# Planning a kernel's streams with a longer issue time for turning DMAs, and a new step order to go with it

## The chip, the cores and the metric

The kernel runs on one core of a Trainium2 chip. The metric is the device time of one execution in microseconds (us). PE is TensorE, PEld its weight load, DVE VectorE, ACT ScalarE, POOL GpSimd, SP SyncE; SPq is SyncE's queue of DMA issues.

## The reference

Linear attention with a learned feature map, whose output is the input of a mixture of eight experts with Sinkhorn-normalised routing:

```python
# batch 8, heads 8, seq 576, head_dim 64, features 128
def phi(x):
    proj = einsum('bhsd,df->bhsf', x, w_phi)
    proj = proj - max(abs(proj), axis=-1, keepdims=True)
    return concatenate([exp(proj), exp(-proj)], axis=-1)
q_p, k_p = phi(q), phi(k)
kv = einsum('bhsf,bhsd->bhfd', k_p, v);  z = sum(k_p, axis=2)
attn = einsum('bhsf,bhfd->bhsd', q_p, kv) / (einsum('bhsf,bhf->bhs', q_p, z) + 1e-6)

x = attn.transpose(0, 2, 1, 3).reshape(4608, 512)
P = exp(x @ w_gate - max)                 # 4608 x 8, then 8 rounds of row and column norms
out = sum over e of P[:, e] * (relu(x @ w1[e]) @ w2[e])     # w1: 8 x 512 x 1024
```

## The kernel before

The kernel holds a planner. Each part of the program calls `plan.op(engine, duration, ...)`; a greedy scheduler with a model of durations and of DMA bandwidth then decides the order in which operations are written into each engine's stream, and which buffer each takes. On the chip each engine works through its stream in the order written, and semaphores decide when the next may start. So a duration in the plan costs nothing on the chip; it only decides an order.

```python
LINK = {..., 230: (470, 108), ..., 148: (265, 30), 160: (540, 50)}      # rate: GB/s, share unit

def dma(queue, nbytes, rate, fn, r=(), w=()):
    speed, unit = LINK.get(rate, (rate, 40))
    if nbytes == 2 << 20:
        speed, unit = 400, 150
    o = plan.op(queue, 0.8 if queue == "POOL" else 0.6, 0.0, fn, r, w, (), nbytes / speed)
    o.turn, o.unit = rate == 148, unit
...
class Links:                              # two lines of transfers: SyncE's and POOL's
    def step(self, t, work):
        ...
        if len(on) == 2:
            a, b = (x[0][2] for x in self.line)
            all_ = (0.61 if a.turn else 0.84) / (a.unit + b.unit)
```

The attention's inputs come in halves of a batch (four heads). POOL loads q and k of a half into one of two `qk` buffers by two DMAs, which also turn fp32 into bf16; SyncE loads v; and one "turning" DMA, `dma_start_transpose`, 512 KB from SBUF to SBUF, turns the half so that the features can be computed. A `qk` buffer is free again when its turn has landed.

```python
ring(a_in, [128, 2, 4, NJ * D], BF16, "qk", 2)       # two buffers
ring(a_t, [128, 2, 8, 128], BF16, "qkT", 3)

def load_qk(b, hh, nh, t, r=()):
    ...
    for x, src in ((1, k), (0, q)):
        dma("POOL", nh << 17, 230, lambda ...: nc.gpsimd.dma_start(
            out=t["qk"]()[:, x, o:o + nh], in_=src[b, hh:hh + nh, 0:SM]...), r, ...)

def turn_qk(t, pr=None):
    ...
        dma("SP", 1 << 19, 148, lambda: nc.sync.dma_start_transpose(
            out=t["T"]()..., in_=t["qk"]()...), ...)
```

Smaller turns of the same kind are `rT` (remainders of the sequence) and `xT` (attention output).

The planner's other input is a string of 322 letters, the order in which the steps are offered to the scheduler: `l` loads a half, `t` turns one, `e` loads remainders, `w` loads weights, `a q p r b n m c` are attention steps, `u` and `d` are up and down parts of expert 0, `g` is a routing gate. Only work up to the last gate is ordered by it; the rest of expert 0 and experts 1 to 7 follow.

The softmax here doesn't subtract the row's maximum and nothing guards it: scores larger than these inputs give would overflow.

Of the kernel before, what the change touches and what calls it, by code (L numbers as in the profile page):

```python
# [119 lines left out]
class Links:  # L120
# [13 lines left out]
    def step(self, t, work):  # L134
        on = [n for n in range(2) if self.line[n] and self.line[n][0][0] <= t + 1e-9]
        later = [x[0][0] for n, x in enumerate(self.line) if x and n not in on]
        if not on:
            return (min(later), None, None) if later else None
        share = [1.0, 1.0]
        if len(on) == 2:  # L140
            a, b = (x[0][2] for x in self.line)
            all_ = (0.61 if a.turn else 0.84) / (a.unit + b.unit)
            share = [all_ * a.unit, all_ * b.unit]
        dt, n = min((work[n] / share[n], n) for n in on)
        if later and later[0] - t < dt:
            dt, n = max(later[0] - t, 0.0), None
        for i in on:
            work[i] -= dt * share[i]
        return t + dt, n, work
# [167 lines left out]
def kernel(  # L317
# [59 lines left out]
    plan = Plan()  # L377
# [17 lines left out]
    def dma(queue, nbytes, rate, fn, r=(), w=()):  # L395

        speed, unit = LINK.get(rate, (rate, 40))
        if nbytes == 2 << 20:
            speed, unit = 400, 150
        o = plan.op(queue, 0.8 if queue == "POOL" else 0.6, 0.0, fn, r, w, (), nbytes / speed)  # L400
        o.turn, o.unit = rate == 148, unit

    TI, GR, KM, QM, PM, NM, RM = 0, 0, 0, 0, 0, 0, 0
# [61 lines left out]
    def load_w(e, r=()):  # L465
        w1, w2 = new("w1"), new("w2")
        for w, src in ((w1, moe_w1), (w2, moe_w2)):
            dma("POOL", 2 << 20, 280, lambda w=w, src=src: nc.gpsimd.dma_start(
                out=w(), in_=src[e].rearrange("(c p) f -> p c f", p=128)),
                r, [(w, i, j) for i in range(2) for j in range(2)])  # L470
        return w1, w2

    def load_w0(i, r):

        w1, w2 = W[0]
        n = i % 4
        if i < 4:
            dma("POOL", 1 << 19, 270, lambda: nc.gpsimd.dma_start(
                out=w1()[:, n, :], in_=moe_w1[0].rearrange("(c p) f -> p c f", p=128)[:, n, :]),
                r, [(w1, n)])  # L480
        else:
            dma("POOL", 1 << 19, 280, lambda: nc.gpsimd.dma_start(
                out=w2()[:, 2 * n:2 * n + 2, :],
                in_=moe_w2[0].rearrange("(c p) f -> p c f", p=128)
                [:, 2 * n:2 * n + 2]), r, [(w2, n)])
# [496 lines left out]
    for b in range(2):  # L982
# [4 lines left out]
        w=["wphi_f0"])  # L987
    dma("ACT", 1 << 15, 100, lambda: nc.scalar.dma_start(out=wphi_f[64:128, :], in_=w_phi),
        w=["wphi_f1"])
# [13 lines left out]
    for i in range(2):  # L1003
        dve(450, lambda i=i: nc.vector.memset(vrd[i], 0.0),
            w=[("vrd", i, h, *y) for h in range(2) for y in ((), (1,))])
# [35 lines left out]
    def stage_g(b):  # L1041
# [9 lines left out]
             "c": lambda j: pair_c(j // 4, j % 4, xbs[j]), "g": stage_g,  # L1051
             "u": lambda i: up0(i // 4, i % 4), "d": lambda i: down0(i // 4, i % 4)}
    order = (
        "lraeaepqbwlqaqawwabwmqlltnrbppnwqbppmrmanbqaqmwwacmpnpbccpwbtcnmqnaqbclupunm"
        "taumquglcapalbcpnqqdcenmucugbblnapmrcqdutabnqpmunpbambccddnqplanmqmducpblttb"
        "augnaqlnrbdcampcadmqeutunqcppmdcaqtdqabpbbmlrqtdnpmuaqualbnagnacctbmqulupran"
        "tdpmtdqcmdnpdabdancpcabbqmpumqbcdgnappqunburqcbugmmnqdcdanumupqbnucmcpnmbddp"
        "bqmpncncubncmmgccg"
    )
    for i, n in enumerate(order):  # L1060
        at[0] = i
# [22 lines left out]
    o = plan.op("X", 0.0, 0.0, swap, w=["late"])  # L1084
# [450 lines left out]
```

## Time and profile before

| | before |
|---|---|
| times, us | 1026.58, 1027.88, 1027.87 |
| span of the profiled execution, us | 1026.8 |
| start of the last gate's 32 matmuls, us from the span's start | 204.83 |
| issue of the 12 big turns, us: mean, median, shortest to longest | 2.62, 1.87, 1.32 to 4.51 |
| least time from a big turn's landing to PE's first use of it (loading it as weights), us | 0.7 |

How to read the views: the page's rows of digits are busy tenths in 40 slices of the span; a windows line is "from:to length, then busy us (count) of PE, PEld, DVE, ACT, POOL, then granted clock, DMA share, GB/s"; a row of waits is "engine, what it wanted, its line <- what ended the wait: us in total, times, longest"; a timeline line is "start, duration, engine, line, operation, output <- input, count, and in brackets how long the engine stood idle before it and what released it".

### The profile page before, as it was taken

The page shows a single profiled execution, that of the slowest core. Times are in us where ns is not written, and L with a number is a line of the kernel's source. Part 1 is how long each engine was busy: PE and PEld are TensorE (multiplying, and loading weights), DVE is VectorE, ACT ScalarE, POOL GpSimd, SP SyncE. Part 2 cuts the span into 40 slices and gives each one's busy share as a digit, 9 for nine tenths or more (in the row PEclk, how much of TensorE's full clock was granted, in tenths as well). Part 3 has the DMA queues.
Part 4 walks back from the last instruction along what each step waited for, and adds up shares of the span by engine and source line. Part 5 has one row for each costly group of instructions (what it writes and reads, how often), then busy time and mean ns, then how long its engine had stood idle before and what let it go on. Part 6 is the DMA issues. An engine that isn't in the chain of part 4 may idle for free.

```text
span 1026.8 us, 24281 instructions
## 1 busy us (share of the span) xinstructions
PE 1008.1 (98%) x9469; PEld 837.9 (82%) x9504; DVE 823.5 (80%) x1600; ACT 703.9 (69%) x1530; POOL 458.5 (45%) x480
## 2 busy tenths in 40 slices
PE   7899999999999999999999999999999999999998
PEld 4666666645888888888888888888888888888886
DVE  7999989987888887787777877787778877787775
ACT  7999999834888766666666666666665666666663
POOL 5768664400334444444444434544444433444342
PEclk9999999999999999999999999999999999999999
DMA  9999978170232611161115211341116111614333
GB/s 235 192 197 179 177 137 130 37 154 19 85 104 85 124 42 42 47 129 43 48 46 112 54 43 42 75 102 42 42 46 131 42 42 43 130 36 125 133 124 124
DMA packets 112501, 96.03 MB, mean 94 GB/s; under 512 B 54145, under 2 KB 87041, under 8 KB 112385
## 3 DMA queue, kind: packets, MB, share of 16 engines
q1 hardware_dynamic: 80576, 70.55, 26.5%
q0 software_dynamic: 31648, 23.86, 16.6%
q8 instruction: 74, 1.21, 0.5%
q14 instruction: 43, 0.34, 0.1%
q10 hardware_dynamic: 160, 0.07, 0.0%
HBM read 94.98 MB, written 14.16 MB: 106 GB/s over the span
## 4 chain that ended last, share of the span: by engine, by line
PE 93%; ACT 2%; DVE 1%; DMA 1%; SPq 1%; issue 1%; POOL 0%; DVEq 0%; ACTq 0%
PE ps L1273 74%; PE ps L573 17%; PE ps L856 2%; DMA acc<-in_q_dram 1%; ACT q L569 1%; ACT k L569 0%; SPq L495 0%; ACT wx L569 0%; SPq L551 0%; PE ps L885 0%; DMA xd<-S 0%; DVE ps L864 0%; DVE hT L1305 0%; DVE m L565 0%; POOL wx L761 0%
## 5 line engine op out<-in xcount | busy, mean ns | idle before, releaser
L1428 POOL TENSOR_TENSOR acc<-acc,V 128x512 f32<-128x512 f32 x248 | 314.8, 1280 | 484.5 <-ACT V L1425 426.7
L1301 ACT COPY U<-ps 128x512 f32<-128x512 f32 x378 | 217.0, 586 | 166.2 <-PE ps L1273 150.9
L1305 DVE CUSTOM_DVE_ANT_0 hT<-ps,U 128x512 bf16<-128x512 f32 x378 | 254.6, 687 | 87.7 <-PE ps L1273 59.9
L1425 ACT ACTIVATE V<-ps,P 128x256 f32<-128x256 f32 x496 | 208.1, 473 | 90.7 <-PE ps L1273 82.1
L1413 DVE SCALAR_TENSOR_TENSOR acc<-ps,P,acc 128x256 f32<-128x256 f32 x372 | 159.1, 478 | 69.5 <-PE ps L1273 69.2
L1273 PEld LDWEIGHTS <-S 128*128 128x128 bf16 x1984 | 194.1, 98 | 22.6 <-issue 0.2
L1273 PEld LDWEIGHTS <-T 128*128 128x128 bf16 x1512 | 148.0, 98 | 17.2
L1273 PEld LDWEIGHTS <-hT 128*128 128x128 bf16 x1488 | 145.6, 98 | 16.8
L1273 PE MATMUL ps<-X,T 128*128 128x256 bf16 x1008 | 152.4, 273 | 0.0
L1273 PE MATMUL ps<-T,S 128*128 128x256 bf16 x1056 | 135.8, 273 | 0.0
L1273 PEld LDWEIGHTS <-wx 128*128 128x128 bf16 x1152 | 112.7, 98 | 13.6 <-issue 0.2
L1181 DVE TENSOR_TENSOR S<-hT 128x1024 bf16<-128x1024 bf16 x124 | 87.2, 712 | 10.1 <-ACT hT L1310 9.9
L1273 PEld LDWEIGHTS <-w 128*128 128x128 bf16 x864 | 84.5, 98 | 9.8
L1273 PE MATMUL ps<-xT,wx 128*128 128x256 bf16 x576 | 88.4, 273 | 0.1
L1273 PE MATMUL ps<-X,wx 128*128 128x256 bf16 x576 | 86.8, 273 | 0.0
L1310 ACT ACTIVATE hT<-ps 128x512 bf16<-128x512 f32 x126 | 73.2, 606 | 9.8 <-PE ps L1273 9.8
L1273 PE MATMUL ps<-wx,hT 128*128 128x256 bf16 x560 | 77.6, 273 | 0.0
L1273 PE MATMUL ps<-xT,T 128*128 128x256 bf16 x504 | 76.7, 273 | 0.0
L573 PE MATMUL ps<-xT,w 128*128 128x512 bf16 x270 | 70.5, 379 | 0.7
L573 PE MATMUL ps<-w,hT 128*128 128x512 bf16 x276 | 69.8, 379 | 0.7 <-ACT q L569 0.2
L1273 PE MATMUL ps<-T,hT 128*128 128x256 bf16 x496 | 69.2, 273 | 0.0
L1273 PE MATMUL ps<-xT,w 128*128 128x256 bf16 x432 | 66.5, 273 | 0.0
(129 smaller groups left out, 1426.5 us busy)
## 6 DMA issues: line engine op xcount, KB each, us to landing
X<-xd SPq DMA_DIRECT2D x126, 256.0 KB, 2.7
wx<-in_moe_w_dram POOLq DMA_DIRECT2D x8, 1024.0 KB, 12.4
v_m<-in_v_dram SPq DMA_DIRECT2D x15, 512.0 KB, 5.6
out_dram<-acc SPq DMA_DIRECT2D x14, 512.0 KB, 2.9
w<-in_moe_w_dram POOLq DMA_DIRECT2D x6, 1024.0 KB, 12.1
xd<-S SPq DMA_DIRECT2D x18, 256.0 KB, 2.1
qk<-in_k_dram POOLq DMA_DIRECT2D x12, 256.0 KB, 5.5
qk<-in_q_dram POOLq DMA_DIRECT2D x12, 256.0 KB, 6.4
```

The lines of the kernel that those rows point to most:

```text
L569: act(el, lambda: nc.scalar.activation(out=dst(), in_=src(), func=ACT.Exp, bias=0.0, scale=scale), r, w)
L573: nc.tensor.matmul(out_, lhsT=lhsT, rhs=rhs, start=start, stop=stop)
L856: pe(65, lambda j=j: nc.tensor.matmul(pn()[:, j * D1:j * D1 + D1], lhsT=s["T"][x]()[:, j % 2, 2 * h + j // 2, :] if j < 4 else r["T"][x]() ...
L1181: lambda: f.tensor_tensor(out=out_(), in0=x(), in1=y(), op=op), r, w, **kw)
L1273: pe(256, lambda i=i, k=k, z=z: nc.tensor.matmul(bank()[:, 256 * i:256 * i + 256], lhsT=lhs(k, i), rhs=rhs(k), start=first and z, stop=k = ...
L1301: act(512, lambda: nc.scalar.copy(out=u[fp][n]().rearrange("p a b -> p (a b)"), in_=x[fp]()), [x[fp]], [u[fp][n]])
L1305: dve(515, lambda: nc.vector._custom_dve(ADD_SAT, out=out_(fp, i, j), in0=bank[fp]().rearrange("p (a b) -> p a b", a=2), in1=u[fp][n](), s ...
L1310: act(512, lambda: nc.scalar.activation(out=out_(fp, i, j), in_=x[fp]().rearrange("p (a b) -> p a b", a=2), func=ACT.Relu, bias=0.0, scale ...
L1413: dve(320, lambda n=n, ts=ts: nc.vector.scalar_tensor_tensor(out=acc[g][:, ts, 256 * j:256 * j + 256], in0=bank()[:, 256 * n:256 * n + 256 ...
L1425: act(370, lambda n=n: nc.scalar.activation(out=u()[:, n, :], in_=bank()[:, 256 * n:256 * n + 256], func=ACT.Copy, bias=0.0, scale=P[:, 4 ...
L1428: pool(695, lambda: nc.gpsimd.tensor_tensor(out=acc[g][:, 2 * i:2 * i + 2, 256 * j:256 * j + 256], in0=acc[g][:, 2 * i:2 * i + 2, 256 * j: ...
```

## The change

Its intent: SyncE spends 1.3 to 4.5 us on issuing a big turn where the plan holds 0.6. So the plan gets 2.4 us for the big ones and 1.25 for the small ones, a smaller share of bandwidth while a turn and a load of POOL are in flight together, and a step string that was searched for with these numbers.

```diff
-            all_ = (0.61 if a.turn else 0.84) / (a.unit + b.unit)
+            all_ = (0.56 if a.turn else 0.84) / (a.unit + b.unit)
...
-        o = plan.op(queue, 0.8 if queue == "POOL" else 0.6, 0.0, fn, r, w, (), nbytes / speed)
+        dur = 0.8 if queue == "POOL" else 0.6 if rate != 148 else 2.4 if nbytes > 1 << 18 else 1.25
+        o = plan.op(queue, dur, 0.0, fn, r, w, (), nbytes / speed)
...
     order = (
-        "lraeaepqbwlqaqawwabwmqlltnrbppnwqbppmrmanbqaqmwwacmpnpbccpwbtcnmqnaqbclupunm"
+        "lraplqabaeenqblwqarwamqwppawwbbmpqapwqnqmbpmnmblltanbtcqccncpwnrlwmlucapunmc"
         ... (four more lines replaced in the same way; the same letters in the same numbers)
```

No instruction is added or removed.

More of the change, by code (lines that the diff above doesn't have):

```diff
@@ L1053 @@
     order = (
-        "lraeaepqbwlqaqawwabwmqlltnrbppnwqbppmrmanbqaqmwwacmpnpbccpwbtcnmqnaqbclupunm"
-        "taumquglcapalbcpnqqdcenmucugbblnapmrcqdutabnqpmunpbambccddnqplanmqmducpblttb"
-        "augnaqlnrbdcampcadmqeutunqcppmdcaqtdqabpbbmlrqtdnpmuaqualbnagnacctbmqulupran"
-        "tdpmtdqcmdnpdabdancpcabbqmpumqbcdgnappqunburqcbugmmnqdcdanumupqbnucmcpnmbddp"
-        "bqmpncncubncmmgccg"
+        "lraplqabaeenqblwqarwamqwppawwbbmpqapwqnqmbpmnmblltanbtcqccncpwnrlwmlucapunmc"
+        "gtupabqttlcbmunnqrbecupaaamdgntqdpmaqdbnlbpqaucaalpqmncuaqubapnecqtmcluabnlb"
+        "pmmduaptndglbqpmdaqcdcrqumtbbqnnpqcacttmdapuqbbupnuclrmmmgdbuqnpqanbdcpqmdua"
+        "cmppqndnbccanduarqtdbgnbpacmqunummddapuqbcpacdqbbpgrcnmubmmuunpbdmqnnpabcmcd"
+        "cndqucpmngbpncmccg"
     )
```

## The prediction

> **What bounds the kernel now.** I read the page first, then the time windows of every engine, then the timeline of SyncE's queue, then the list of waits, and at the end the start times of the matmuls. The times of before are 1026.58, 1027.88 and 1027.87 us, so the scatter is about 1.3 us and 2% is 20.6 us.
>
> The page's rows of busy time show three stages. Columns are 40 slices of 25.7 us.
>
> ```profile
> span 1026.8 us, 24281 instructions
> PE   7899999999999999999999999999999999999998
> DVE  7999989987888887787777877787778877787775
> ACT  7999999834888766666666666666665666666663
> PEclk9999999999999999999999999999999999999999
> ```
>
> In slices 2 to 8 (to about 206 us) TensorE, VectorE and ScalarE are all nearly full: this is the attention, mixed with the first part of expert 0. Then ScalarE falls to 3 for two slices: the routing table is made and the rest of expert 0 runs. From slice 10 on experts 1 to 7 run with TensorE always busy at the full granted clock. The windows give the same with numbers (length, then busy us of PE, PEld, DVE, ACT, POOL):
>
> ```profile
> 0.00:50.00 50.00, 38.49 (x398) 26.97 (x400) 43.54 (x90) 43.39 (x109) 31.59 (x58) 1.00 1.15 212
> 50.00:206.00 156.00, 153.69 (x1833) 102.77 (x1861) 143.73 (x340) 147.27 (x358) 101.68 (x163) 1.00 0.90 143
> 206.00:253.00 47.00, 46.77 (x233) 22.46 (x236) 35.96 (x94) 18.18 (x32) 0.62 (x1) 1.00 0.39 85
> 253.00:1027.00 774.00, 769.15 (x7010) 685.69 (x7009) 600.32 (x1078) 495.04 (x1034) 324.63 (x260) 1.00 0.30 76
> ```
>
> The reader should see that 774 of 1027 us lie behind 253 us, where TensorE alone decides; the step order that is changed there is none. What can move is the first 206 us. In that stretch the busy shares of three engines are 92 to 98%, so no single wait carries it.
>
> What SyncE does in that stretch is in its queue's timeline (start, duration, instruction). [...]
>
> ```profile
> 45.39 6.37 SPq L518 DMA_TRANSPOSE qkT<-qk  x2
> 84.84 1.36 SPq L518 DMA_TRANSPOSE qkT<-qk  x1
> 100.38 1.19 SPq L879 DMA_TRANSPOSE xT<-wx  x1
> 116.00 4.51 SPq L518 DMA_TRANSPOSE qkT<-qk  x1
> 141.24 0.37 SPq L509 DMA_DIRECT2D v_m<-in_v_dram  x1
> 171.84 1.69 SPq L518 DMA_TRANSPOSE qkT<-qk  x1
> ```
>
> A plain load costs SyncE 0.37 to 1 us, a turning DMA of a 128 x 512 tile 1.19, and one of 128 x 2048 from 1.32 to 4.51 (the twelve have a mean of 2.6 and a median of 1.87). The plan of before holds 0.6 for all of them. So 34 turning DMAs (12 big, 6 of rT, 16 of xT) take about 12 x 2.6 + 6 x 2.1 + 16 x 1.27 = 64 us of SyncE where the plan thought 20.
>
> Did that hurt? In the list of waits up to 206 us, these are all the rows in which a compute engine's wait was ended by a DMA for 0.2 us or more:
>
> ```profile
> PE ps L703 <- DMA acc<-in_k_dram: 3.7, 1, 3.7
> PEld L573 <- DMA rT<-qk_r: 1.7, 1, 1.7
> ACT wgate L1009 <- DMA wgate_f<-in_moe_w_gate_dram: 0.6, 1, 0.6
> DVE wphi L995 <- DMA wphi_f<-in_w_phi_dram: 0.6, 1, 0.6
> PE ps L703 <- DMA acc<-in_q_dram: 0.3, 1, 0.3
> POOL wx L759 <- DMA xT<-xb: 0.2, 1, 0.2
> ```
>
> The first is the first load of the program. Only rT (1.7 us) and xT (0.2 us) are turning DMAs that came too late for a compute engine, 1.9 us together. SyncE's own waits are long, but its queue has slack: 64 us of issuing in the 165 us from 27 to 192 us.
>
> **What the Trainium skill says.** "DMA: Bandwidth & Descriptors", section "DMA Transpose (X-bar)": the plain DMA transpose can only be issued by Sync or Scalar. That fits the program: every turning DMA stands in SyncE's queue, and there is one queue in which a slow issue delays the v loads behind it. The same page, section "Issuing engines are not separate DMA queues", says that the sequencer's time to start a DMA is usually small against the DMA itself. The trace doesn't agree for turning DMAs: 1.2 of 3.2 us (xT) and a median of 1.87 of 5.9 us from issue to landing (qkT), a third of it. "Trainium Kernel Development and Optimization", section "Performance Expectations", calls matmul busy time a bad metric of the distance to roofline, because matmuls are pipelined. The trace agrees: a 128 x 512 matmul is shown as 379 ns, but 49 of them start in 10.35 us, 211 ns each. So I count TensorE by start-to-start times and not by its 98%.
>
> **The change part by part.** (1) Two durations of SyncE's issue in the plan (2.4 us for the 512 KB turn, 1.25 for the smaller ones) and one bandwidth share (0.56 in place of 0.61). None of this is an instruction; it only changes in what order the planner writes operations into each engine's stream and which buffer and bank each takes. Cost on the chip: 0.
> (2) The string of 322 steps. Both strings have the same letters in the same numbers (32 pairs, 24 up and 20 down parts of expert 0, 12 big turns, 14 half loads, 8 weight loads). The built programs have the same number of instructions on each engine, of the same kinds: PE 18938, DVE 1602, ACT 1534, POOL 485, SP 252. So work removed 0, added 0, all moved. The streams differ from PE instruction 21, DVE 10, ACT 12, SP 19 on; by line and shape the last 462 of ACT, 518 of DVE and 4794 or more of PE are the same again: all from expert 1 on, the 774 us.
>
> What is moved, as work in front of landmarks, with start-to-start times of the trace (512 columns 0.215 us, 256 columns 0.109, 65 columns 0.029; ScalarE 0.476 per 512 elements; VectorE 0.6 per 512 from PSUM):
> - In front of the last gate: PE 179.9 us before, 180.5 after (three more up matmuls); ACT 181.0 in both, with the same 52 relus and 10 copies; VectorE 177 in both. That gate runs at 205.2 us, so about 25 us of each engine are idle in front of it, and behind it the same 47 us of expert 0 cover the routing. The change is worth exactly what it takes from, or adds to, these 25 us.
> - Of PE's idle time in front of the gate, 20.7 us lie in the first 50 us (29.3 us of work there, by the start times), where there is no xT yet to feed expert 0. The first up matmul has 25.9 us of PE work and 39.9 us of ACT work in front of it before, 26.4 and 40.7 after: ScalarE, which is the full engine there, gets 0.8 us more to do first. So this part is +0.3 to +0.8 us.
> - From 50 to 206 us PE loses some 10 us in many small pieces. There the new order spreads expert 0 more evenly. PE work between every 24 up matmuls was 11.6, 18.8, 19.7, 27.4, 9.7, 28.6, 13.5, 18.9 and is 11.5, 22.1, 13.0, 23.7, 19.3, 18.9, 19.1, 19.9. More even filler between work that waits for ScalarE should save a part of the 10 us; I take a quarter at most, -2.5 to 0.
> - The turning DMAs that came late: 1.9 us at most, and part of it would be hidden behind other work; -1 to 0.
> - The fourth quarter of expert 0's first weight is issued with 25.2 us of POOL work in front of it (19.6 before, when it was issued at 35.35 us). I estimate issue at 38 to 41 us; with the page's 7.7 us from issue to landing it lands at 46 to 49, and PE needs it with 28.0 us of work in front of it, so at about 48.5. That is 0 to +1 us.
> Sum of the middles: +0.5 - 1.25 - 0.5 + 0.3 = about -1 us, and with 1027.5 as the centre of before, 1026.5 us.
>
> **The rivals.** (a) The wrong issue times were what made SyncE's queue late and the whole attention slow; then the new order wins several us, to about 1020. For it: 64 us against 20 is a large error, and the queue is in order. Against it: compute engines waited 1.9 us for turning DMAs. (b) The new order is best in the plan alone, and on the chip the streams, which are in order on each engine, meet other waits (a weight that lands late, a bank not yet free), each of which holds three engines; 1029 to 1032. For it: the order is searched against a model with errors as large as the one it now repairs. Against it: the order of before came from the same kind of search and shows few waits. (c) The two orders are two equal solutions, and the difference is within 1 us: 1027 to 1028. (d) The freed time is eaten behind the gate: not likely, since PE is busy 46.77 of 47 us there, so an earlier gate shifts everything.
>
> **Range and chances.** The floor is set by ScalarE: 181 us of work in front of the gate plus about 4 us until its first data, against 205; even a perfect order can't win 20 us, so over 2% faster is next to impossible, and a loss of 20 us would need a new stall almost as long as all idle time there is. From rivals (a) and (b), each with a fifth, the range for 8 in 10 is 1022.5 to 1030.0 us. Chances: faster 0.005, within 2% 0.985, slower 0.01.
>
> **What would show it.** Right: the matmuls from expert 1 on start earlier or later by the same amount as the end; in the windows the stage 253 to 1027 keeps its 774 us; the last gate runs between 202 and 208 us; SyncE's turning DMAs keep 1.2 and about 1.9 us, since the plan's numbers don't change the chip; the waits that DMA end stay under 3 us beside the first load. Wrong: the gate moves by over 5 us, a wait of PE for a weight or a turn of over 2 us appears near 48 us or later, or experts 1 to 7 change in length.

## More of the kernel before

POOL, the engine that issues the q and k loads, also computes: it multiplies v by the features' scale and, before that, negates a small table of maxima (`m_r`, `m`) that ScalarE's next exponential reads.

```python
pool(8, lambda: nc.gpsimd.tensor_scalar_mul(m()[:, 1], m()[:, 2], -1.0), mk, [(m, "neg")])
exp(10, lambda: em(), lambda: m()[:, 1:3], 1.0, mk + [(m, "neg")], [em])
```

The profiled execution of before took 1028.55 us, a little more than the timed ones.

## The result, and the profile after

| | before | after |
|---|---|---|
| median of six runs, us | 1027.2 (1026.36 to 1027.88) | 1030.46 (1029.23 to 1031.09) |
| ratio to before | | 1.003, 95% 1.0017 to 1.0043 |
| span of the profiled execution, us | 1026.8 | 1028.8 |
| start of the last gate's 32 matmuls, us | 204.83 | 206.58 |
| issue of the 12 big turns, us: mean, median, range | 2.62, 1.87, 1.32 to 4.51 | 3.47, 3.27, 1.70 to 6.77 |

The changed kernel is 0.3% slower: within 2%, but 0.46 us above the range that I gave, and its interval excludes 1.

From the page of after, the rows of busy tenths of DVE and ScalarE:

```profile
DVE  7989998887888887788777877787778877787775
ACT  7989998934878766666656666666666666666663
```

In slice 3, which is 51 to 77 us, both fall from 9 to 8; ScalarE also has an 8 in slice 7 where it had a 9. From slice 11 on, where experts 1 to 7 run, the rows differ by one digit in one place (DVE) and in three (ScalarE). In the page's chain of what ended last, PE has 90% of the span where it had 93%. DMA has 3% where it had 1%, and the page's next line gives 2% of them to a turning DMA (`qkT<-qk`) and 1% to a load of q into its buffer (`qk<-in_q_dram`), neither of which was named in the chain before. That names the suspects, no more: time in the chain is not time lost.

Where the time went is shown by short windows. In before:

```profile
65.00:80.00 15.00, 14.68 (x172) 9.81 (x174) 14.10 (x34) 14.19 (x36) 9.01 (x14) 1.00 1.14 192
125.00:150.00 25.00, 24.79 (x267) 15.63 (x269) 23.15 (x53) 24.56 (x65) 17.41 (x32) 1.00 0.82 148
```

In after:

```profile
65.00:80.00 15.00, 13.13 (x136) 8.16 (x137) 12.69 (x29) 12.37 (x31) 11.22 (x19) 1.00 1.43 191
125.00:150.00 25.00, 23.89 (x282) 16.03 (x286) 22.48 (x54) 23.19 (x58) 14.76 (x25) 1.00 1.18 177
```

In the 15 us from 65 us PE loses 1.55 us of busy time against before, DVE 1.41 and ScalarE 1.82, all three at once; POOL is busier by 2.2. In the second window PE loses 0.90, DVE 0.67 and ScalarE 1.37. Elsewhere after is not behind: PE is busy 1.0 us longer in the first 50 us. From the last gate to the end both take nearly the same (821.9 and 822.2 us), so what is lost in front of the gate is lost at the end.

What ended the waits in the first 206 us, where before had no wait of a compute engine for `qkT` or `qk` of 0.2 us or more, is in these rows of after:

```profile
POOL qk L502 <- DMA qkT<-qk: 3.4, 2, 1.7
PEld L574 <- DMA qkT<-qk: 2.3, 2, 1.3
ACT em_r L570 <- POOL m_r L679: 2.0, 2, 1.4
PE ps L574 <- DMA qkT<-qk: 1.9, 2, 1.0
```

PE waits twice for a turn, about 1 us each. POOL waits twice to issue a load of q and k, because the turn that frees the buffer has not landed. ScalarE waits for POOL's negation `m_r`. SyncE's queue in after shows why:

```profile
54.56 0.37 SPq L510 DMA_DIRECT2D v_m<-in_v_dram  x1
56.01 10.05 SPq L519 DMA_TRANSPOSE qkT<-qk  x2
...
129.33 6.21 SPq L519 DMA_TRANSPOSE qkT<-qk  x1
```

The line with x2 holds two issues, of 6.77 and 3.11 us in the trace; the turns land at 66.40 and 69.64 us. The turn of 129.33 takes 6.21 us to issue and lands at 139.04. The plan held 2.4 us for each. What stood waiting, on PE, POOL and ScalarE of after:

```profile
66.45 0.61 PE L574 MATMUL ps<-wphi,qkT 128*128 128x256 bf16 x4 [1.03 <-DMA qkT<-qk]
139.09 1.05 PE L574 MATMUL ps<-wphi,qkT 128*128 128x256 bf16 x8 [0.84 <-DMA qkT<-qk]
```

```profile
66.93 0.77 POOL L502 DMA_DIRECT2D qk<-in_k_dram  x1 [1.69 <-DMA qkT<-qk]
...
70.17 0.74 POOL L502 DMA_DIRECT2D qk<-in_k_dram  x1 [1.72 <-DMA qkT<-qk]
...
71.67 0.25 POOL L679 TENSOR_SCALAR m_r<-m_r 128x4 f32<-128x4 f32 x1
```

```profile
71.95 0.21 ACT L570 ACTIVATE em_r<-m_r 128x8 f32<-128x8 f32 x1 [1.42 <-POOL m_r L679]
```

Read from below: ScalarE stands 1.42 us for a 0.25 us negation, which stands in POOL's stream behind four loads that cost 0.75 us each, two of which waited for late turns. Two turns have no slack at all in after (66.40 landed, 66.45 used; 139.04 and 139.09). The smallest slack of the others is 3.6 us, and two small turns that are issued ahead of the late one at 129 us have 21 and 39 us. Before, the smallest slack of a big turn is 0.7 us (landed at 51.72, loaded as weights at 52.39) and the next 3.4: one turn was nearly late there too, but none was.

### The profile page after: what moved, and what is told of

Read it like the earlier page. It is cut to its first block, busy times and chain, and to the rows that moved or that the text cites. A ratio compares the mean times of both kernels' runs of the same rounds, so it can differ in the third digit from the quotient of the medians.

```text
span 1028.8 us, 24264 instructions
## 1 busy us (share of the span) xinstructions
PE 1008.5 (98%) x9466; PEld 837.4 (81%) x9504; DVE 822.7 (80%) x1600; ACT 704.0 (68%) x1530; POOL 458.2 (45%) x480
## 4 chain that ended last, share of the span: by engine, by line
PE 90%; ACT 3%; DMA 3%; DVE 1%; issue 1%; POOL 1%; SPq 0%; DVEq 0%; ACTq 0%; POOLq 0%
PE ps L1274 74%; PE ps L574 15%; DMA qkT<-qk 2%; PE ps L857 1%; ACT wx L570 1%; ACT k L570 1%; DMA qk<-in_q_dram 1%; ACT q L570 0%; DMA acc<-in_q_dram 0%; ACT qr L570 0%; ACT kr L570 0%; ACT qkT L712 0%; SPq L552 0%; POOL qk_r L557 0%; DVE S L1182 0%
```

## The experiments

**Theories.** The one I held first (theory A in the expectations): the new order leaves two turns with little slack, and as their issue takes longer than the plan's 2.4 us they come late and delay PE. Rivals: the new order is worse by itself, late turns or not (its first 50 us, its filler; theory B); the new numbers alone spoil the plan (theory C in the expectations); and two that came up on the way: the length of an issue is set by what else is in flight, so that no constant fits (theory D), and the loss runs through POOL's in-order stream to ScalarE rather than through PE's own wait (theory E).

**How the edits are made.** After the planner has made its list, a step moves single operations of SyncE or POOL within their streams; (queue, n, m) moves the n-th in front of the m-th. It refuses a move that breaks a dependence or the order of uses of a buffer. PE's, DVE's and ScalarE's streams stay those of the kernel edited.

```diff
+    MOVES = [("SP", 35, 34), ...]
+    def moved(self, done):
+        lists = {q: [o for o in done if o.eng == q] for q in ("POOL", "SP")}
+        for q, n, m in self.MOVES:
+            o, p = lists[q][n], lists[q][m]
+            done.remove(o)
+            done.insert(done.index(p), o)
+        ...                                    # asserts on dependences and buffer order
     def run(self, tc):
-        done = self.schedule()
+        done = self.moved(self.schedule())
```

All twelve kernels gave correct results. "Gate" is the start of the last gate's last matmul in the one profiled execution, "rest" what follows to the end.

| run | median us | before beside it | ratio to before, 95% | gate | rest |
|---|---|---|---|---|---|
| before | 1027.2 | | | 205.6 | 821.2 |
| after | 1030.46 | 1027.2 | 1.003 (1.0017 to 1.0043) | 207.4 | 821.4 |
| newplan_oldstring | 1028.45 | 1027.31 | 1.0004 (0.9988 to 1.0019) | 203.6 | 821.1 |
| oldplan_newstring | 1038.78 | 1026.98 | 1.0114 (1.0101 to 1.0127) | 214.9 | 820.9 |
| after_s1 | 1033.3 | 1027.31 | 1.0055 (1.004 to 1.007) | 210.3 | 820.9 |
| after_s1b | 1029.94 | 1027.31 | 1.0024 (1.0009 to 1.0039) | 208.5 | 820.9 |
| after_s12 | 1034.18 | 1027.31 | 1.0066 (1.005 to 1.0082) | 210.4 | 821.4 |
| after_m | 1030.49 | 1026.98 | 1.0031 (1.0019 to 1.0043) | 208.1 | 820.9 |
| after_msp | 1028.62 | 1026.98 | 1.0014 (1.0002 to 1.0026) | 205.0 | 821.4 |
| after_buf | 1027.85 | 1026.98 | 1.0006 (0.9995 to 1.0018) | 205.8 | 820.7 |
| after_sp | 1028.84 | 1026.97 | 1.0018 (1.0005 to 1.0032) | 207.5 | 821.4 |
| after_buf_sp | 1025.82 | 1026.97 | 0.9986 (0.9974 to 0.9999) | 204.0 | 820.6 |
| after_quiet | 1026.15 | 1026.97 | 0.9991 (0.9978 to 1.0003) | 204.8 | 820.6 |
| before_late | 1032.36 | 1026.97 | 1.0043 (1.0028 to 1.0057) | 210.2 | 821.1 |

The rest lies between 820.6 and 821.4 us in all fourteen profiles: nearly everything that the change and the experiments do to the time happens in front of the gate. A gate time comes from one execution, though, and executions differ: newplan_oldstring, which is nearly the program of before, had its gate 2.0 us earlier in its profile, and that execution took 1026.54 us where the profiled one of before took 1028.55. ScalarE, with the same stream, was 1.2 us ahead at 30 us and 1.6 at 50 us.

### newplan_oldstring: the numbers alone

The new durations and share with the string of before. The built program differs from before in two neighbouring issues of SyncE that are exchanged.

```diff
 (before, with the two hunks of numbers of the change; the string left as it was)
```

> The new numbers in the plan with the old step string. In the built program only two neighbouring SyncE issues change places, so this is the kernel of before but for that. Theory A (the new string's late big turns cost the time) and B (the new string's order of compute work costs it) both say 1027 to 1028 us, ratio to before 0.999 to 1.001. Theory C (the numbers in the plan do the harm, by delaying what SyncE issues) says 1029.5 to 1031.

Measured: ratio 1.0004, its interval spans 1. The numbers alone do nothing that these runs show; theory C falls. One turn of this run was issued in 5.91 us (at 114.00 us), and it still landed 3.1 us before PE needed it: with slack behind it, a long issue cost nothing here.

### oldplan_newstring: the string alone

```diff
 (before, with the new string; the numbers left as they were)
```

> The new string with the old numbers (0.6 us for every issue, share 0.61): the plan sets 1039 of PE's 18938 instructions and 104 of ScalarE's otherwise than with the new numbers. If the new string is only good with the numbers it was found for, this is slower than the changed kernel, 1031 to 1036 us; if the numbers do not matter, 1029.5 to 1031.5.

Measured: 1038.78 us, ratio 1.0114, the slowest of all. Under the old numbers the new string makes another program (1039 PE and 104 ScalarE instructions are placed otherwise). The two rows of waits that stand out, and what they are on the chip, from the waits of this run:

```profile
POOL qk L501 <- DMA qkT<-qk: 4.1, 1, 4.1
ACT wx L569 <- POOL wx L759: 3.8, 1, 3.8
```

POOL holds a load for a late turn for 4.1 us, and ScalarE waits 3.8 us for a small operation of POOL. So string and numbers are a pair: a string found for one set of numbers is not good with another. It does not tell how much of these 11 us is the late turn, since so much else moved and two stretches at half the clock (from 40.97 and 71.69 us, 3.41 us each) fall into this profile.

### after_s1, after_s1b, after_s12: earlier turns

after_s1 brings the first of the two late turns forward: its pair of q and k loads goes ahead of a multiplication of v in POOL's stream, two weight loads go behind, and the turn goes ahead of a v load in SyncE's queue. after_s1b does the last of these alone. after_s12 is after_s1 with the same done for the late turn at 129 us.

```diff
+ after_s1:  MOVES = [("POOL", 51, 49), ("POOL", 52, 49), ("POOL", 46, 55), ("POOL", 48, 55), ("SP", 35, 34)]
+ after_s1b: MOVES = [("SP", 35, 34)]
+ after_s12: MOVES = after_s1's + [("POOL", 138, 132), ("POOL", 139, 132), ("SP", 61, 58)]
```

> The changed kernel with one spot mended: the pair of q/k loads issued by POOL at 48.6 us goes about 2 to 4 us earlier (two weight loads go behind), and its big turn goes ahead of the v load in SyncE's queue. No compute instruction changes its place on any engine. In the changed kernel PE waited for that turn at 66.45 us, and ScalarE fell about 3 us behind the plan there. Theory A: the wait at 66 us is gone, the turn lands by 63 us, the stretch 65 to 80 us gets back 2 us of PE, total 1027.5 to 1028.8 us. Theory B: the wait is gone and the time stays at 1030 to 1031, since other waits take its place. Theory D (a turn's issue takes as long as what runs beside it makes it, not a constant): the issue of that turn falls from 6.8 to under 5 us.

> The changed kernel with one exchange in SyncE's queue alone: the big turn at 56 us goes ahead of the 512 KB v load that was issued at 54.6. The q/k loads stay where they were. Theory D (contention with transfers in flight sets the length of the issue): issue falls from 6.8 to about 4.5 us and the landing from 66.4 to about 64, total 1028 to 1029.5. If the lateness of the q/k load alone matters: the issue still starts at about 56, takes over 6 us, and the total stays 1030 to 1031.

> Both spots mended: as the first, and near 117 us the q/k pair goes ahead of the four small q/k loads of the remainder on POOL, and the big turn that landed at 139.0 us ahead of the two small turns on SyncE. Theory A: PE's wait at 139.1 us (1.0 us) goes too, ScalarE's lag there (1.2 us) too, total 1026.3 to 1027.8 us, at or under before. Theory B: 1029.5 to 1031.

Two clear misses: after_s1 and after_s12 are slower than after. PE's wait at 66 us is gone in both. But the first turn, which now starts at 51.94 us beside loads in flight, takes 8.14 us to issue, and the second turn after it 5.01. SyncE and POOL in after_s1:

```profile
51.94 8.14 SPq L543 DMA_TRANSPOSE qkT<-qk  x1
...
60.88 5.01 SPq L543 DMA_TRANSPOSE qkT<-qk  x1
```

```profile
71.97 0.74 POOL L526 DMA_DIRECT2D qk<-in_k_dram  x1 [5.14 <-DMA qkT<-qk]
...
73.46 0.25 POOL L703 TENSOR_SCALAR m_r<-m_r 128x4 f32<-128x4 f32 x1
```

POOL stands 5.14 us in front of a load; its stream runs in order, so what it could compute behind the load stands too, and ScalarE waits up to 4.3 us for `m_r`. Compared instruction by instruction, ScalarE is 1.8 us behind after at 72 us and 3.2 us from 81 us on. The second step has a further cause: PE stood idle for 3.5 us up to 75.21, and from 75.82 on the granted clock was half for 3.41 us. The window has it as 0.66:

```profile
75.00:80.00 5.00, 4.79 (x26) 2.21 (x26) 3.77 (x10) 3.45 (x10) 4.72 (x9) 0.66 1.47 208
```

Half the clock for 3.41 us takes at most 1.7 us of PE's work (my estimate), and all runs of after_s1 and after_s12 have a mean clock of 0.996 to 0.998, where those of after have 0.999 or 1.0. So a part of the loss of both, up to 1.7 of some 2.6 and 3.7 us by the ratios, can be this slow stretch, and the rest is the waiting. This is where theory E came from: the first theory, by PE's wait alone, would have made the run faster. after_s12 removes PE's wait at 139 us, worth 1.0 us, and loses 1.4 at 124 us, where its q and k loads now stand ahead of a multiplication of v that others wait for.

after_s1b is inconclusive in the total (1029.94, its range 1028.74 to 1031.93 covers the median of after). In its profile the issue falls from 6.77 to 5.14 us and ScalarE gains 0.9 us at 66 to 72 us; the late turn at 140 us is as late as ever (PE waits 1.4 us). The profiled execution began with a stretch at half the clock (from 11.01 us); the four runs with a mean clock of 0.999 or 1.0 took 1028.74 to 1030.52 us, the two at 0.998 took 1031.22 and 1031.93.

### after_m: the negation ahead of the loads

If POOL's held loads hurt only through `m_r`, it is enough to put that one operation of POOL in front of them.

```diff
+ MOVES = [("POOL", 81, 77)]
```

> What the run with the loads moved showed: POOL issues its queue in order, and there it stood 5.1 us at a q/k load that waited for the big turn to free its buffer, with a 0.25 us negation behind it (128 x 4, for the remainder) that ScalarE waits for. In the changed kernel the same stands: POOL waits twice 1.7 us at 66 and 70 us, the negation runs at 71.67, ScalarE loses 1.4 us. Here that negation alone goes ahead of the four blocked loads on POOL; no other instruction moves. Theory E (POOL's queue, held by a load that waits for a late turn, holds ScalarE): negation at 65 to 67 us, ScalarE's wait gone, ScalarE 1 to 1.5 us earlier from 72 us to the end, total 1028.8 to 1029.6 us. Theory B (order of compute work): no gain, 1030 to 1031.

Measured: 1030.49, no gain, a miss. The negation ran at 65.59 us, and ScalarE gained 1.85 us on after between 65 and 72.5 us. Then the next small operation behind the same loads held ScalarE:

```profile
75.31 0.22 ACT L594 ACTIVATE em<-m 128x16 f32<-128x16 f32 x1 [1.07 <-POOL m L784]
```

And the late turn of the second spot was issued in 6.91 us, and PE's longest wait for a turn grew to 1.7 us. One symptom removed, the cause left in place.

### after_msp, after_sp: the two exchanges on SyncE

Each late turn goes ahead of items with slack in SyncE's queue: the first ahead of a v load, the second ahead of three items, two of them small turns. after_msp has the negation moved as well.

```diff
+ after_sp:  MOVES = [("SP", 35, 34), ("SP", 61, 58)]
+ after_msp: MOVES = [("POOL", 81, 77), ("SP", 35, 34), ("SP", 61, 58)]
```

> The negation ahead of the blocked loads, and two exchanges in SyncE's queue: the big turn of 56 us ahead of the v load before it (which alone gave 0.9 us between 66 and 72 us), and the big turn of 129 us ahead of the two small turns before it. Compute engines keep their order but for that negation. Theories D and E together: 1.4 + 0.9 + 1.0 us back, total 1026.8 to 1028.2, equal to before. Theory B: 1029.5 to 1031.

> The changed kernel with the two exchanges in SyncE's queue alone (the big turn of 56 us ahead of the v load, the one of 129 us ahead of the two small turns); no instruction of another engine moves. The run that also moved the negation gave 1028.6. If the negation counts for nothing (as it did by itself), the same here, 1028 to 1029.2; both of PE's waits for a big turn (66 and 139 us) are under 0.3 us, and the second turn's issue falls from 6.2 to about 3.6 us. If the negation was part of the gain: 1029.2 to 1030.

after_msp: 1028.62, after_sp: 1028.84, 0.16 and 0.12% under after by their ratios, whose intervals overlap that of after. In both PE's waits for turns are gone. In after_sp the loss at 65 to 80 us has moved to POOL. Its waits:

```profile
POOL qk L526 <- DMA qkT<-qk: 3.7, 1, 3.7
ACT em_r L594 <- POOL m_r L703: 3.4, 2, 2.8
```

The first pair of loads now finds its buffer free, and the second pair still waits, for longer, with `m_r` behind it. (This profiled execution, at 1030.7 us, also has a stretch at half the clock, from 73.92 us, after PE had stood idle for 2.1 us. The three runs of after_sp with a mean clock of 0.999 or 1.0 took 1028.66 to 1028.84, the two at 0.997 and 0.998 took 1030.7 and 1030.87.) So the turns' lateness at PE and the loads' waiting on POOL are two ways in which the same lateness gets through, and closing one opens the other.

### after_buf: two more buffers

The four loads at 65 to 72 us are given two more `qk` buffers, laid into a part of an accumulator tile that is not in use yet. No order changes.

```diff
+        for n, slot in ((77, 2), (79, 3)):
+            for b in lists["POOL"][n].bufs:
+                b.slot = slot
...
+    qk_make = R["qk"].make
+    R["qk"].make = lambda i: qk_make(i) if i < 2 else acc[4]...[:, 2048 * (i - 2):2048 * (i - 1)]...
```

> The changed kernel with two more q/k buffers (in an accumulator that is idle until expert 0's fifth group) for the two pairs of loads that POOL was held by; every order as in the changed kernel. Theory E: POOL's two waits of 1.7 us and ScalarE's 1.4 us are gone, total 1028.5 to 1029.6. Theory D adds: the loads now run beside the two big turns, whose issues take longer still (over 6.8 and 3.1 us), PE's wait for the first turn (1.2 us at 66 us) grows, and part or all of the gain is lost: 1029 to 1030.5. Theory B: 1030 to 1031 with both waits gone.

Measured: 1027.85, ratio to before 1.0006. POOL's waits for `qk` and ScalarE's long wait for `m_r` are gone, ScalarE is 1.5 to 1.7 us ahead of after. The issues of the late turns are as long as ever (6.70, 3.07 and 7.27 us) and PE waits 0.7 us for each of the two late ones.

### after_buf_sp: both

```diff
+ MOVES = [("SP", 35, 34), ("SP", 61, 58)], and the two buffers of after_buf
```

> The two exchanges in SyncE's queue and the two more q/k buffers together. If late turns and the loads that wait for their buffers are the whole cause: 1.5 to 2 us from the buffers, and 1 us from the turn of 139 us on top, total 1026.0 to 1027.3, equal to before or a little under it, since the changed kernel led by 1.5 to 2 us until 65 us. If something else in the new string costs time: 1027.5 to 1029.

Measured: 1025.82 (1025.64 to 1026.44), ratio 0.9986 with an interval that just ends under 1. This is the fastest of all and beats both kernels, before by little: 0.14% by the ratios, and 4.5 us under after (1.003 less 0.9986, of 1027). PE, DVE and ScalarE have the same streams as after. SyncE:

```profile
55.78 5.05 SPq L550 DMA_TRANSPOSE qkT<-qk  x1
...
61.63 3.45 SPq L550 DMA_TRANSPOSE qkT<-qk  x1
```

```profile
126.54 3.72 SPq L550 DMA_TRANSPOSE qkT<-qk  x1
```

and POOL:

```profile
68.17 0.29 POOL L710 TENSOR_SCALAR m_r<-m_r 128x4 f32<-128x4 f32 x1
```

The turn that landed at 139.04 us lands at 133.43, and POOL's negation comes at 68.17 in place of 71.67. No wait of PE or POOL for a turn is left. The same two windows as above:

```profile
65.00:80.00 15.00, 14.84 (x177) 10.05 (x177) 14.79 (x36) 14.26 (x37) 12.67 (x21) 1.00 1.41 208
...
125.00:150.00 25.00, 24.79 (x271) 16.15 (x272) 23.74 (x57) 24.10 (x61) 14.81 (x27) 1.00 1.17 175
```

PE gets back 1.71 us in the first and 0.90 in the second, 2.6 together; ScalarE is 2.4 us ahead of after from 72 us on and 3.46 from 141 us on. Of the remaining 1.1 us between 3.46 and the 4.5 of the ratios, 0.8 lies behind the gate in these two profiles (821.4 and 820.6 us), where nothing was edited, and 0.3 is not placed. The first 50 us are not it: ScalarE is 0.05 us ahead at 65 us. No run gave before the two buffers; its trace has no wait of POOL for a turn of 0.2 us or more that they could remove.

### after_quiet: is the issue time a constant?

The edit of after_buf_sp, with two loads of q and k on POOL moved from in front of the turn of 126 us to behind it.

```diff
+ MOVES = after_buf_sp's + [("POOL", 141, 155), ("POOL", 144, 155)]
```

> As the run before, and the q/k loads that POOL starts at 124.2 and 127.5 us go behind the big turn of 128 us, so that less runs beside it. Theory D (what is in flight sets the issue's length): its issue falls from about 3.6 to under 2.5 us. If the issue has a fixed length of about 2.4 us as the plan holds: 2.4 to 3.6 as without. Total within 1 us of the run before.

```profile
127.08 1.92 SPq L550 DMA_TRANSPOSE qkT<-qk  x1
```

The same turn is issued in 1.92 us where it took 3.72, and 6.21 in after. So what is in flight sets a part of the length of an issue (theory D holds for this turn), and no number in the plan can be right for all. The total didn't move (1026.15): the turn had slack by then, and the loads that were moved fell beside the next two turns, whose issues in the trace grew from 1.76 and 1.97 to 5.68 and 4.50 us.

### before_late: a late turn put into before

The opposite test: the turn that before issues at 116.0 us goes behind five items of SyncE's queue. Nothing else changes.

```diff
 (before)
+ MOVES = [("SP", 54, 60)]
```

> The kernel of before made worse in the suspected way: in SyncE's queue the big turn of 116.0 us goes behind two v_r loads, a small turn, the next big turn and a v load. It had 6.6 us between landing (124.2) and PE's first use (130.8). Now it should be issued at about 127 and land at 131.5 to 134. Theory A: PE waits 0.5 to 3 us for it, the total rises by most of that, to 1027.5 to 1030. If a late turn is covered by other work: 1026.5 to 1027.5 in spite of the wait.

Measured: 1032.36, ratio 1.0043, slower than I had expected. The turn is issued at 125.60 us, in 4.00 us, and lands at 131.71. PE's timeline:

```profile
131.75 1.04 PE L597 MATMUL ps<-wphi,qkT 128*128 128x256 bf16 x4 [3.30 <-DMA qkT<-qk]
```

PE waits 3.3 us for it; ScalarE loses 5.9 us between 131.5 and 135.3 us, and the gate and the end move with it. ScalarE loses more than PE waits because PE came back at half the clock: it was granted half from 130.61 us on for 6.83 us. A window of the run, and PE in it:

```profile
130.00:138.00 8.00, 6.25 (x55) 3.79 (x56) 3.18 (x8) 2.62 (x8) 2.58 (x4) 0.57 0.40 85
```

```profile
132.58 3.62 PE L597 MATMUL ps<-xT,w 128*128 128x512 bf16 x8
```

The starts of these eight matmuls lie 0.427 us apart, where 0.215 is usual. From 131.75 to 137.44 us that costs PE some 2.8 us (my estimate), which with the wait of 3.3 accounts for about the 5.9. The runs agree: the two with a mean clock of 0.999 or 1.0 took 1030.09 and 1030.20, the three at 0.997 and 0.998 took 1032.36 to 1033.28; the runs of before beside them at 0.999 or 1.0 have a mean of 1027.28. So the late turn by itself costs 2.9 us, in a program where all else is before's, and the slow clock after it 2.8 more where it came. (The turn had 5.5 us of slack in before, used at 129.70, not the 6.6 of the expectation.)

What brings the slow clock was not tested. Five such stretches, in after_s1, after_s12, after_sp, before_late and oldplan_newstring, begin between 1.2 us before and 0.9 us after the end of a wait of PE of 2.1 to 4.0 us. But oldplan_newstring has another one, at 40.97 us, with no wait over 0.6 us in the 14 us before it. In after PE's longest wait for a turn is 1.03 us and no such stretch follows.

## Why the prediction was wrong

The number was 0.46 us above the range, and its sign was wrong: about -1 us was predicted and +3.3 came.

- **The step that failed** is the term "The turning DMAs that came late: 1.9 us at most, ... -1 to 0". It counted the lateness that the trace of before shows and that the new order could remove. It left out that the new order makes its own. The term measured +3.4: after_buf_sp, with the same streams of the compute engines but no late turn, has ScalarE 2.4 us ahead from the first spot on and 1.0 more after the second. By the total it is up to 4.5.
- **Why it failed.** I had the numbers in hand: issues of 1.32 to 4.51 us, with a median of 1.87 and the plan's new value at 2.4. I read the new value as a repair. But the two late turns were issued in 6.77 and 6.21 us, 4.4 and 3.8 above the plan's number. My estimate is that at 2.4 us they would have landed some 3.3 and 3.0 us ahead of PE's need (those excesses less PE's waits of 1.03 and 0.84 us): enough for the plan, not for the chip. In before the least slack left was 0.7 us after an issue of 4.32 us, so its margin had been thinner than the plan of after held: that its turns came in time was partly luck. The new order also packs four q and k loads behind each other, with two buffers, so that POOL is held as well. The slack of each turn (landing against first use) and POOL's queue behind a held load were not in my working.
- **"SyncE's turning DMAs keep 1.2 and about 1.9 us, since the plan's numbers don't change the chip"** was wrong for the big ones: median 3.27. The numbers don't change the chip, the order does, by what it puts beside a turn (after_quiet: 3.72 to 1.92 us by moving two loads).
- **"The waits that DMA end stay under 3 us beside the first load"** failed: PE 1.9, PEld 2.3, POOL 3.4 us. It was a fit sign of the failure, as intended. The sign named for being wrong, a wait of PE of over 2 us for a turn, did not come: the longest was 1.03 us, since a part of the loss went through POOL.
- **Rival (b)**, 1029 to 1032 us by other waits, is what happened. I named a weight and a bank as what would be late; it was a turn and POOL. I gave it a fifth and too little of the range.
- **Filler, -2.5 to 0, and the first 50 us, +0.3 to +0.8:** not shown either way. With the late turns away the kernel is 0.14% under before, so these two and the two exchanges come to about -1.4 us together, which doesn't contradict the terms. The 2 us by which profiled executions differ are too much to separate them.
- **Slips in the working** that don't explain the miss: the middle of 0 to +1 was entered as 0.3 (with 0.5 the sum is -0.7); idle times of 20.7 and 10 us don't fit into 25; 49 starts in 10.35 us are 48 steps, so 216 ns each; ScalarE's row has a 3 and a 4, not two 3s; and plain loads of 512 KB took up to 2.29 us to issue (68.36 us), not 1, so uneven issues were to be seen there too.
- **The weight's fourth quarter, 0 to +1:** no wait of PE for a weight appears in after. It was 0.
- **What held:** the same instructions, nothing changed behind the gate (821.2 and 821.4 us), the gate between 202 and 208 us, the end moving by about what the gate moves (2.0 and 1.75 us in the profiles), and the chance of a change over 2%.

What stays open: what within SyncE's queue or the DMA engines makes an issue long. POOL's loads in flight are part of it, by after_quiet; but before has turns that were issued in 1.32 and 1.36 us (at 66.93 and 84.84 us) while such loads were in flight and nothing of SyncE's own. Transfers of SyncE's own are not needed for a long one: the 8.14 us of after_s1 came with five loads of POOL in flight and none of SyncE's. Open too are the scatter of the first 50 us and what brings the stretches at half the clock.

## What to carry to other kernels

When a planner's constants are made more exact, look at the slack that the new order leaves, not only at the lateness that the old one shows: a duration that varies between 1.3 and 8 us has to be planned with a margin, or what depends on it needs room. Put the transfer without slack ahead of those with slack in the same queue, and give an engine that both computes and issues loads one more buffer, so that it never stands in front of a load while another engine waits for the small operation behind it. When a wait is taken away and the time stays, read the waits again before giving up the theory: here the loss moved from PE to POOL and back until both ways were closed. And look at the granted clock of each profile: it explained here what the waits could not.

## What the Trainium skill lacked or had wrong

- "DMA: Bandwidth & Descriptors", section "Issuing engines are not separate DMA queues", calls the time of initiating a DMA "usually small relative to the DMA itself". For a 512 KB turn within SBUF it was 1.3 to 6.8 us in before and after, against 4.3 to 10.4 us from issue to landing.
- The same page, section "DMA Transpose (X-bar)", gives no issue time for such a turn, and not that it depends on what is in flight (the page's part on trn3 has a count of sequencer cycles for earlier chips, but no time, and nothing of what is in flight): the same turn was issued in 6.21, 3.72 and 1.92 us in three orders of the streams.
- "Perfetto Trace Analysis", section "What \"DMA-bound\" means", says that the window shown on the issuing sequencer's track is descriptor generation; the section that it refers to counts a wait for a lock in it as well, without a size. The 12 big turns are of one size and shape, and their windows differ by a factor of 4 in one profile (1.70 to 6.77 us), so more than the work of generating sets the window's length; the runs do not show what.
- No page that I read says what a load issued by GpSimd costs the computing behind it: 0.74 to 0.84 us per load of q or k here, and, where its buffer wasn't free, up to 5.14 us in which POOL's stream stood, so that ScalarE waited 4.3 us for an operation of 0.25 us (after_s1).
